# A list scheduler, single PSUM banks and 64x64 transposes in an attention and adapter kernel

## The chip, the core and the metric

The kernel runs on one core of one Trainium2 chip. The metric is the device time of one execution in microseconds (us). Five engines matter: PE multiplies matrices and writes PSUM, ACT and DVE read PSUM and do the elementwise work, POOL starts the loads, SP starts the stores. Each runs its own instructions strictly in the order in which the program gives them, and waits on semaphores for the others. PSUM has eight banks, each of 512 float32 numbers in each of 128 partitions.

## What is computed

Attention with a squared ReLU in place of the softmax (8 batches, 12 heads, 448 rows, head width 64), and behind it a mixture of eight low-rank adapters (rank 16) on the 3584 rows of 768 numbers that it gives; each row takes the two adapters with the highest gate.

```python
scores = scale * np.matmul(q, k.transpose(0, 1, 3, 2))
attn = np.maximum(scores, 0.0) ** 2 / S
x = np.matmul(attn, v)                  # then (b, s, h * d): 3584 x 768
...
logits = x @ w_gate                     # 768 -> 8
topk = np.argpartition(-logits, K, axis=1)[:, :K]          # K = 2
w = np.exp(sel); w /= w.sum(-1, keepdims=True) + 1e-09
delta[mask] += w[mask, k, None] * ((x[mask] @ A[e]) @ B[e])
out = x + delta
```

## The kernel before

**Tiling.** Two heads from each half of the twelve form a quad, so there are three quads for each batch and 24 in all. A quad's keys are cut into seven blocks of 64 rows. One block of one quad is a *slot*; there are 168. In a slot PE multiplies a block of k with all of q for four heads (`emit_qk`, L228: four 64x64 matmuls of 448 columns, which sit in the four quarters of the array), ACT takes the ReLU of the two banks of scores in one instruction of 896 columns (`emit_relu`, L238), DVE squares it (L240), and PE multiplies by v and adds into two banks `oT` (`emit_pv`, L252, four 64x64 matmuls again). After seven slots `emit_xt` copies the two banks as bf16 into `xt` (ACT L262, DVE L263), which holds the attention's result transposed.

**Transposes.** q and k of the next quad are turned by `job_transpose`: 14 matmuls against an identity, each on 128 rows and 64 columns (L112), into one bank, which DVE copies out at once (L119, 896 bf16 columns). There is one such job for q and one for k of each quad, 48 in all.

**Adapters.** `job_moe` handles two or three 128-row tiles at a time, twelve groups for 28 tiles: six matmuls for each tile give gate and first adapter factor (L133), a chain of small DVE instructions with one ACT exponential makes the weights (L145 to L166), a transpose (L175) and a copy (L180) turn the weighted factor, and for each tile two output parts of 512 and 256 columns follow: identity matmuls that bring x back (L189), the second factor in float32 (L197), the copy out (ACT L208, DVE L210), the store (SP L212).

**Order.** The loop over slots writes it out by hand: `emit_qk`, then one step of a transpose job or of `job_moe` (each `yield` ends a step), then `emit_relu`, then `emit_pv` of the slot two before (`LAG = 2`). A batch's adapter work begins when its last quad is copied out; what is left of it when the slots end is run behind them.

**Buffers.** The scores have two tiles of two banks, `oT` two banks, and transposes, gates and outputs share two banks (`ps_m`). A batch's loads go out on POOL's queue two batches ahead, in three tiles; the first batch's are cut into two slots' worth each.

Of the kernel before, what the change touches and what calls it, by code (L numbers as in the profile page):

```python
# [12 lines left out]
ALU = mybir.AluOpType  # L13

J = 7
PH = 64


@with_exitstack
def kernel(  # L20
# [21 lines left out]
    NC_ = HH // 2  # L42
    scale = 1.0 / math.sqrt(Dh)
# [3 lines left out]
    loads = ctx.enter_context(tc.tile_pool(name="loads", bufs=3))  # L47
    tpool = ctx.enter_context(tc.tile_pool(name="tpool", bufs=2))
    apool = ctx.enter_context(tc.tile_pool(name="apool", bufs=4))
    mpool = ctx.enter_context(tc.tile_pool(name="mpool", bufs=2))  # L50
    opool = ctx.enter_context(tc.tile_pool(name="opool", bufs=4))
    ps_s = ctx.enter_context(tc.tile_pool(name="ps_s", bufs=2, space=bass.MemoryType.PSUM))
    ps_o = ctx.enter_context(tc.tile_pool(name="ps_o", bufs=1, space=bass.MemoryType.PSUM))
    ps_m = ctx.enter_context(tc.tile_pool(name="ps_m", bufs=2, space=bass.MemoryType.PSUM))
# [5 lines left out]
    identb = const.tile([128, 128], BF16)  # L60

# [5 lines left out]
    )  # L67

    batches = {}

    def load_batch(b, per_quad=False):
        tiles = [
            loads.tile([128, HH, J * Dh], BF16, name=f"{nm}n{b}", tag=f"{nm}n") for nm in "qkv"
        ]
        batches[b] = tiles
        parts = [(2 * c, 2 * c + 2) for c in range(NC_)] if per_quad else [(0, HH)]
        for s0, s1 in parts:
            for t, src in zip(tiles, (qv, kv, vv)):
                for g in range(2):
                    nc.gpsimd.dma_start(  # L80
                        out=t[g * PH : g * PH + PH, s0:s1, :], in_=src[b, g, :, s0:s1, :]
                    )
# [3 lines left out]
    load_batch(0, per_quad=True)  # L86
    nc.sync.dma_start(out=B_sb, in_=moe_B.rearrange("e r d -> (e r) d"))
    load_batch(1)
    nc.gpsimd.dma_start(
        out=awg[:, :, RE:ZW], in_=moe_w_gate.rearrange("(do di) e -> di do e", di=128)  # L90
    )
    for do in range(DO):
        nc.gpsimd.dma_start(
            out=awg[:, do, 0:RE].rearrange("p (e r) -> p e r", e=E),
            in_=moe_A[:, do * 128 : do * 128 + 128, :].transpose([1, 0, 2]),
        )

    quads = [(b, c) for b in range(B) for c in range(NC_)]
    NQ = len(quads)
    qkT = {}  # L100

    def misc(name):
        return ps_m.tile([128, 512], F32, name=name, tag="misc")


    def job_transpose(qi, which):
        b, c = quads[qi]
        src = batches[b][which]
        ps = ps_m.tile([128, J * 128], BF16, name=f"tp{which}_{qi}", tag="misc")
        for j in range(J):  # L110
            for sl in range(2):
                nc.tensor.transpose(  # L112
                    ps[sl * PH : sl * PH + PH, j * 128 : j * 128 + 128],
                    src[:, 2 * c + sl, j * Dh : j * Dh + Dh],
                    identb,
                )
        yield
        sb = tpool.tile([128, J, 2, PH], BF16, name=f"{'qk'[which]}T{qi}", tag=f"{'qk'[which]}T")
        nc.vector.tensor_copy(sb.rearrange("p j a s -> p (j a s)"), ps)  # L119
        qkT[qi, which] = sb  # L120

    def out_rows(m, bp):

        b = 2 * bp + m // J
        return out[b * S : b * S + S, :].rearrange("(p j) f -> j p f", j=J)[m % J]

    def job_moe(bp, tiles_):
        T = len(tiles_)
        c0 = [bp * 2 * S + 128 * i for i in tiles_]
        z = misc(f"z{bp}_{tiles_[0]}")  # L130
        for t in range(T):
            for do in range(DO):
                nc.tensor.matmul(  # L133
                    out=z[:, t * ZW : t * ZW + ZW],
                    lhsT=xt[:, do, c0[t] : c0[t] + 128],
                    rhs=awg[:, do, :],
                    start=(do == 0),
                    stop=(do == DO - 1),
                )
        yield  # L140
        z3 = z[:, : T * ZW].rearrange("p (t w) -> p t w", t=T)
        lg = z3[:, :, RE:ZW]
        mx = mpool.tile([128, 3, 8], F32, name=f"mx{bp}_{tiles_[0]}", tag="mx")
        for t in range(T):
            nc.vector.max(mx[:, t, :], z[:, t * ZW + RE : t * ZW + ZW])  # L145
        sub = mpool.tile([128, 3, E], F32, name=f"sub{bp}_{tiles_[0]}", tag="sub")
        nc.vector.tensor_tensor(
            sub[:, :T], lg, mx[:, :T, 0:1].to_broadcast([128, T, E]), op=ALU.subtract
        )
        w = mpool.tile([128, 3, E], F32, name=f"w{bp}_{tiles_[0]}", tag="w")  # L150
        nc.scalar.activation(w[:, :T], sub[:, :T], ACTF.Exp)
        mask = mpool.tile([128, 3, E], F32, name=f"mask{bp}_{tiles_[0]}", tag="mask")
        nc.vector.tensor_tensor(
            mask[:, :T], lg, mx[:, :T, 1:2].to_broadcast([128, T, E]), op=ALU.is_ge
        )
        yield
        nc.vector.tensor_mul(w[:, :T], w[:, :T], mask[:, :T])
        ws = mpool.tile([128, 3], F32, name=f"ws{bp}_{tiles_[0]}", tag="ws")
        nc.vector.reduce_sum(ws[:, :T], w[:, :T], axis=mybir.AxisListType.X)
        nc.vector.reciprocal(ws[:, :T], ws[:, :T])  # L160
        nc.vector.tensor_tensor(
            w[:, :T], w[:, :T], ws[:, :T, None].to_broadcast([128, T, E]), op=ALU.mult
        )
        zp = mpool.tile([128, 3, E, R], F32, name=f"zp{bp}_{tiles_[0]}", tag="zp")
        for t in range(T):
            nc.vector.tensor_tensor(  # L166
                zp[:, t],
                z[:, t * ZW : t * ZW + RE].rearrange("p (e r) -> p e r", e=E),
                w[:, t, :, None].to_broadcast([128, E, R]),
                op=ALU.mult,  # L170
            )
        yield
        zt = misc(f"zt{bp}_{tiles_[0]}")
        for t in range(T):
            nc.tensor.transpose(  # L175
                zt[:, t * 128 : t * 128 + 128], zp[:, t].rearrange("p e r -> p (e r)"), identf
            )
        yield
        zT = mpool.tile([128, 3 * 128], F32, name=f"zT{bp}_{tiles_[0]}", tag="zT")
        nc.scalar.copy(zT[:, : T * 128], zt[:, : T * 128])  # L180
        yield
        pend = None
        for t in range(T):
            osb = opool.tile([128, D], F32, name=f"o{bp}_{tiles_[t]}", tag="o")
            for part in range(2):
                d0, nd = (0, 4) if part == 0 else (4, 2)
                o = misc(f"o{part}_{bp}_{tiles_[t]}")
                for i in range(nd):
                    nc.tensor.matmul(  # L189
                        out=o[:, i * 128 : i * 128 + 128],  # L190
                        lhsT=xt[:, d0 + i, c0[t] : c0[t] + 128],
                        rhs=identb,
                        start=(i == 0),
                        stop=False,
                        skip_group_check=True,
                    )
                nc.tensor.matmul(  # L197
                    out=o[:, : nd * 128],
                    lhsT=zT[:, t * 128 : t * 128 + 128],
                    rhs=B_sb[:, d0 * 128 : (d0 + nd) * 128],  # L200
                    start=False,
                    stop=True,
                    skip_group_check=True,
                )
                yield
                dst = osb[:, d0 * 128 : (d0 + nd) * 128]
                if part == 0:
                    nc.scalar.copy(dst, o[:, : nd * 128])  # L208
                else:
                    nc.vector.tensor_copy(dst, o[:, : nd * 128])  # L210
                    for hh in range(2):
                        nc.sync.dma_start(  # L212
                            out=out_rows(2 * tiles_[t] + hh, bp),
                            in_=osb[hh * PH : hh * PH + PH, :],
                        )


    sc, at2, oT = {}, {}, {}

    def emit_qk(n):  # L220
        qi, j = divmod(n, J)
        qT, kT = qkT[qi, 0], qkT[qi, 1]
        s = ps_s.tile([128, 2, 512], F32, name=f"s{n}", tag="s")
        sc[n] = s
        for sl in range(2):
            r0 = sl * PH
            for a in range(2):
                nc.tensor.matmul(  # L228
# [118 lines left out]
```

## Time and profile before

| | before |
|---|---|
| median of 3 runs | 277.51 us (277.43 to 278.75) |
| the profiled execution | 275.26 us |
| its span | 273.5 us |
| busy: PE, ACT, DVE | 205.1, 177.7, 169.2 us |
| first ReLU starts | 9.94 us |
| last v matmuls start | 249.55 us |
| mean granted TensorE clock | 0.931 of 2.4 GHz |

An engine's busy time counts an instruction from its start to its end, and instructions that follow closely on one engine overlap, so what an instruction holds up its engine for is read from the distance between two starts where nothing waits. Lines as L238 are lines of the kernel before; `a<-s` reads "writes a, reads s".

### The profile page before, as it was taken

The numbers are of one execution on the slowest core, as the hardware profiler recorded it, in microseconds if no ns is written. First come the engines' busy times: TensorE is split into PE (matmuls) and PEld (weight loads), VectorE is DVE, ScalarE is ACT, GpSimd is POOL, SyncE is SP. The second block draws the span as 40 slices with busy tenths as digits, with TensorE's granted clock in tenths as the row PEclk, the third lists the DMA queues.
The fourth block names the chain that finished last, engine by engine and source line by source line (L and its number), as shares of the span: only waits on it lengthen the run. The fifth ranks groups of instructions, "written<-read, shape, count | busy, mean of one in ns | idle before, by whom it ended". The sixth has DMA issues, their size and how long they took to land.

```text
span 273.5 us, 6096 instructions
## 1 busy us (share of the span) xinstructions
PE 205.1 (75%) x2492; PEld 100.3 (37%) x2492; DVE 169.2 (62%) x397; ACT 177.7 (65%) x245; POOL 45.2 (17%) x73
## 2 busy tenths in 40 slices
PE   0877759976795997898697687788686866789762
PEld 0433424433343344434344334334233433334331
DVE  0588866586867657756877767755746666463230
ACT  1488957786786576767777787676736776664120
POOL 8975732101110103001110100000000000000000
PEclk9999997999999599599999999799959979979799
DMA  7999999998193188716692642022200400403244
GB/s 130 186 181 182 112 203 205 220 228 139 21 211 89 9 149 145 119 37 123 128 188 72 112 97 60 2 59 60 59 2 6 111 0 2 115 2 84 89 116 115
DMA packets 31067, 28.51 MB, mean 104 GB/s; under 512 B 8896, under 2 KB 27328, under 8 KB 31040
## 3 DMA queue, kind: packets, MB, share of 16 engines
q0 software_dynamic: 26416, 16.73, 49.3%
q1 hardware_dynamic: 4624, 11.41, 15.4%
q8 instruction: 19, 0.31, 0.5%
q14 instruction: 8, 0.07, 0.1%
HBM read 33.84 MB, written 11.01 MB: 164 GB/s over the span
## 4 chain that ended last, share of the span: by engine, by line
PE 44%; DVE 21%; ACT 19%; issue 8%; POOL 4%; DMA 2%; ACTq 0%; POOLq 0%
ACT a L238 15%; PE o L197 15%; PE oT L252 10%; DVE a L240 9%; PE s L228 7%; PE o L189 6%; ACT o L208 3%; DVE kT L119 3%; DMA qn<-in_q_dram 2%; DVE xt L263 2%; PE tp L112 2%; PE zt L175 2%; DVE zp L166 2%; POOL qn L80 2%; PE z L133 2%
## 5 line engine op out<-in xcount | busy, mean ns | idle before, releaser
L238 ACT ACTIVATE a<-s 128x896 bf16<-128x896 f32 x168 | 148.6, 921 | 43.9 <-PE s L228 42.9
L240 DVE TENSOR_TENSOR a<-a 128x896 bf16<-128x896 bf16 x168 | 103.5, 623 | 76.0 <-ACT a L238 74.7
L252 PE MATMUL oT<-a,vn 64*64 64x448 bf16 x672 | 71.6, 390 | 13.5 <-DVE a L240 4.8
L228 PE MATMUL s<-qT,kT 64*64 64x448 bf16 x672 | 68.0, 381 | 10.9 <-ACT a L238 10.2
L197 PE MATMUL o<-B_sb,zT 128*128 128x512 f32 (+1 forms) x112 | 53.0, 559 | 0.5 <-ACT zT L180 0.5
L252 PEld LDWEIGHTS <-vn 64*64 64x64 bf16 x672 | 23.5, 108 | 61.2 <-issue 49.8
L228 PEld LDWEIGHTS <-kT 64*64 64x64 bf16 x672 | 24.3, 112 | 18.9 <-issue 14.9
L189 PE MATMUL o<-identb,xt 128*128 128x128 bf16 x168 | 20.5, 236 | 12.0 <-ACT o L208 8.3
L208 ACT COPY o<-o 128x512 f32<-128x512 f32 x28 | 16.5, 589 | 16.6 <-PE o L197 16.6
L189 PEld LDWEIGHTS <-xt 128*128 128x128 bf16 x168 | 12.3, 104 | 34.3 <-issue 29.5
L80 POOL DMA_DIRECT2D vn<-in_v_dram x20 | 13.0, 666 | 64.7 <-PE s L228 46.0
L112 PE MATMUL tp<-identb,qn 128*64 128x128 bf16 x336 | 15.8, 241 | 6.6 <-DMA qn<-in_q_dram 6.6
L197 PEld LDWEIGHTS o<-B_sb,zT 128*128 128x128 f32 x112 | 18.8, 210 | 0.8 <-ACT zT L180 0.8
L175 PE MATMUL zt<-identf,zp 128*128 128x128 f32 x28 | 7.2, 354 | 15.2 <-DVE zp L166 15.2
L119 DVE COPY qT<-tp 128x896 bf16<-128x896 bf16 x24 | 14.8, 615 | 5.8 <-PE tp L112 5.8
L210 DVE COPY o<-o 128x256 f32<-128x256 f32 x28 | 11.7, 418 | 10.6 <-PE o L197 10.6
L80 POOL DMA_DIRECT2D qn<-in_q_dram x20 | 13.2, 671 | 30.4 <-PE tp L112 28.6
L112 PEld LDWEIGHTS <-qn 128*64 128x64 bf16 x336 | 11.6, 121 | 15.7 <-issue 8.4
L133 PE MATMUL z<-awg,xt 128*128 128x136 bf16 x168 | 12.7, 223 | 4.3 <-DVE kT L119 2.4
L263 DVE CAST xt<-oT 128x448 bf16<-128x448 f32 x24 | 14.8, 618 | 1.7 <-PE oT L252 1.7
L112 PE MATMUL tp<-identb,kn 128*64 128x128 bf16 x336 | 15.1, 233 | 0.3 <-DMA kn<-in_k_dram 0.3
L119 DVE COPY kT<-tp 128x896 bf16<-128x896 bf16 x24 | 14.8, 618 | 0.6 <-PE tp L112 0.6
(25 smaller groups left out, 89.6 us busy)
## 6 DMA issues: line engine op xcount, KB each, us to landing
out_dram<-o SPq DMA_DIRECT2D x56, 192.0 KB, 2.7
qn<-in_q_dram POOLq DMA_DIRECT2D x14, 336.0 KB, 6.5
kn<-in_k_dram POOLq DMA_DIRECT2D x14, 336.0 KB, 7.5
vn<-in_v_dram POOLq DMA_DIRECT2D x14, 336.0 KB, 6.0
qn<-in_q_dram POOLq DMA_DIRECT2D x6, 112.0 KB, 4.5
kn<-in_k_dram POOLq DMA_DIRECT2D x6, 112.0 KB, 4.5
vn<-in_v_dram POOLq DMA_DIRECT2D x6, 112.0 KB, 4.7
B_sb<-in_moe_B_dram SPq DMA_DIRECT2D x1, 384.0 KB, 3.3
```

Source lines behind the costliest of these rows:

```text
L80: nc.gpsimd.dma_start(out=t[g * PH : g * PH + PH, s0:s1, :], in_=src[b, g, :, s0:s1, :])
L112: nc.tensor.transpose(ps[sl * PH : sl * PH + PH, j * 128 : j * 128 + 128], src[:, 2 * c + sl, j * Dh : j * Dh + Dh], identb,)
L119: nc.vector.tensor_copy(sb.rearrange("p j a s -> p (j a s)"), ps)
L133: nc.tensor.matmul(out=z[:, t * ZW : t * ZW + ZW], lhsT=xt[:, do, c0[t] : c0[t] + 128], rhs=awg[:, do, :], start=(do == 0), stop=(do == DO ...
L189: nc.tensor.matmul(out=o[:, i * 128 : i * 128 + 128], lhsT=xt[:, d0 + i, c0[t] : c0[t] + 128], rhs=identb, start=(i == 0), stop=False, ski ...
L197: nc.tensor.matmul(out=o[:, : nd * 128], lhsT=zT[:, t * 128 : t * 128 + 128], rhs=B_sb[:, d0 * 128 : (d0 + nd) * 128], start=False, stop=True,
L208: nc.scalar.copy(dst, o[:, : nd * 128])
L228: nc.tensor.matmul(out=s[a * PH : a * PH + PH, sl, 0:S].rearrange("p (j s) -> p j s", j=J), lhsT=kT[r0 : r0 + PH, j, a, :], rhs=qT[r0 : r0 ...
L238: nc.scalar.activation(a1, sc[n][:, :, 0:S], ACTF.Relu, scale=relu_scale)
L240: nc.vector.tensor_mul(a2, a1, a1)
L252: nc.tensor.matmul(out=oT[qi][g][sl * PH : sl * PH + PH, 0:S], lhsT=vn[r0 : r0 + PH, 2 * c + sl, j * Dh : j * Dh + Dh], rhs=at2[n][r0 : r0 ...
L263: nc.vector.tensor_copy(xt[:, NC_ + c, b * S : b * S + S], oT[qi][1][:, 0:S])
```

## The change

The slots' loop is replaced by a list of operations with their costs, engines, buffers and PSUM banks; a planner (`schedule`) runs through it once when the program is built, and the instructions are issued in the order of its planned start times. The chip still runs a fixed order.

- **Planner.** It keeps a time for each engine, picks ready operations, prefers q-k matmuls, then v matmuls and transposes of the form 64x64, and puts adapter work (`mode="128"`) between where the planned ReLUs cover it. Copies out of PSUM go to ACT or DVE, whichever is free.
- **Banks.** One PSUM tile of eight banks; four are for scores, four for all else, given and returned one by one. The ReLU of a slot is two instructions of 448 columns, each of which returns its bank.
- **Transposes.** 28 matmuls of 64x64 for each job in place of 14 of 128x64, in the four quarters of the array, into two banks; two DVE copies of 448 columns in place of one of 896.
- **Adapters.** Ten groups (eight of three tiles, two of two) in place of twelve. The zp product is one DVE instruction for a group. Output: each pair of tiles has three banks of 512 columns and three copies out, and the second factor goes in pieces of 256 columns (84 in place of 56 matmuls). Stores are 63 in place of 56 DMAs.
- **Last batch.** Its rows are cut into two halves of 224 columns with 21 slots each, so there are 147 whole and 42 half slots.
- **Loads.** The second batch is loaded in parts too. The adapters' first factor comes in rows of 96 numbers and PE puts it in place with a selection matrix (72 small matmuls).

```diff
+BANKS = {"s": [0, 1, 2, 3], "m": [4, 5, 6, 7]}
+DEFER = 3
...
+        att = sorted(
+            (o for o in c if o.mode == "64" and not (o.kind == "tp" and o.rank > next_q)),
+            key=lambda o: (o.kind == "pv", o.kind == "tp", seq[id(o)]),
+        )
+        late = [o for o in c if o.kind == "tp" and o.rank > next_q]
+        fill = [o for o in c if o.mode != "64"]
+
+        cover = max(free["ACT"], t) + sum(o.dur["ACT"] for o in relus)
+        if mode == "64" and att:
+            return att[0]
+        if fill:
+            f = fill[0]
+            if not att or att[0].kind != "qk" or t + f.dur[e] + switch + 0.55 <= cover + SLACK:
+                return f
+        return (att or fill or late)[0]
...
+    ps = psum.tile([128, 8, 512], F32)
...
+        def mm():
+            for j in range(J):
+                for g in range(2):
+                    r = slice(g * PH, g * PH + PH)
+                    for sl in range(2):
+                        nc.tensor.transpose(
+                            bank(m, g).bitcast(BF16)[sl * PH : sl * PH + PH, j * PH : j * PH + PH],
+                            T[b, w][r, 2 * c + sl, j * Dh : j * Dh + Dh],
+                            identb[r, r],
+                        )
...
+        r0 = op(ACT, act(W), AL, lambda: fn(0), deps=[qk_ops[n]], after=prev, kind="relu",
+                take=("a1",), free=[(qk_ops[n], 0)])
+        r1 = op(ACT, act(W), AL, lambda: fn(1), deps=[qk_ops[n]], after=r0, kind="relu", free=[(qk_ops[n], 1)])
...
+    for o in schedule(ops):
+        o.fn()
...
-    LAG = 2
-    run(job_transpose(0, 0))
-    run(job_transpose(0, 1))
...
-        if n < total:
-            emit_relu(n)
-        if 0 <= n - LAG < total:
-            emit_pv(n - LAG)
-    for g in todo:
-        run(g)
```

**The first group of gates on DVE.** Here `a2` is a slot's square, `kT` a transposed k, `mx` to `zp` the gate chain. Before:

```order
L240 TENSOR_TENSOR a2_24_662<-a1_24_660 128x896
L119 COPY kT4_673<-tp1_4_645 128x896
L145 MAX mx0_0_675<-z0_0_611 128x8 x3
L147 TENSOR_TENSOR sub0_0_679<-z0_0_611,mx0_0_675 128x24
L153 TENSOR_TENSOR mask0_0_683<-z0_0_611,mx0_0_675 128x24
L240 TENSOR_TENSOR a2_25_687<-a1_25_685 128x896
L157 TENSOR_TENSOR w0_0_681<-w0_0_681,mask0_0_683 128x24
L159 TENSOR_REDUCE ws0_0_699<-w0_0_681 128x3
L160 RECIPROCAL ws0_0_699<-ws0_0_699 128x3
L161 TENSOR_TENSOR w0_0_681<-w0_0_681,ws0_0_699 128x24
L166 TENSOR_TENSOR zp0_0_703<-z0_0_611,w0_0_681 128x128 x3
L240 TENSOR_TENSOR a2_26_709<-a1_26_707 128x896
```

The same group on DVE after the change:

```order
L497 MAX mx_0_940<-ps_91 128x8 x3
L428 TENSOR_TENSOR a2_26_948<-a1_26_918 128x896
L504 TENSOR_TENSOR sub0_965<-ps_91,mx_0_940 128x24
L513 TENSOR_TENSOR mask0_967<-ps_91,mx_0_940 128x24
L428 TENSOR_TENSOR a2_27_973<-a1_27_938 128x896
L520 TENSOR_TENSOR wt0_979<-wt0_979,mask0_967 128x24
L523 TENSOR_REDUCE ws0_989<-wt0_979 128x3
L428 TENSOR_TENSOR a2_28_991<-a1_28_963 128x896
L528 RECIPROCAL ws0_989<-ws0_989 128x3
L463 CAST xt_92<-ps_91 128x448
L532 TENSOR_TENSOR wt0_979<-wt0_979,ws0_989 128x24
L428 TENSOR_TENSOR a2_29_1036<-a1_29_987 128x896
```

One square stood inside the chain before; four stand between its links now.

**The same group's exponential on ACT** (`w`, now `wt`), among the ReLUs (`a1`). Before:

```order
L238 ACTIVATE a1_23_630<-s23_604 128x896
L238 ACTIVATE a1_24_660<-s24_640 128x896
L151 ACTIVATE w0_0_681<-sub0_0_679 128x24
L238 ACTIVATE a1_25_685<-s25_668 128x896
L238 ACTIVATE a1_26_707<-s26_693 128x896
L238 ACTIVATE a1_27_724<-s27_715 128x896
L180 COPY zT0_0_737<-zt0_0_720 128x384
```

On ACT after the change, where "x2" marks the two halves of a slot:

```order
L413 ACTIVATE a1_24_879<-ps_91 128x448 x2
L413 ACTIVATE a1_25_901<-ps_91 128x448 x2
L413 ACTIVATE a1_26_918<-ps_91 128x448 x2
L413 ACTIVATE a1_27_938<-ps_91 128x448 x2
L413 ACTIVATE a1_28_963<-ps_91 128x448
L510 ACTIVATE wt0_979<-sub0_965 128x24
L413 ACTIVATE a1_28_963<-ps_91 128x448
L413 ACTIVATE a1_29_987<-ps_91 128x448 x2
```

The exponential stood one ReLU behind the maxima's inputs; it now stands four slots further on, and the zT copy has left this stretch of ACT for DVE.

**The end of PE's list.** Before, behind the last v matmul (L252), there are 24 gate matmuls, 4 transposes, 30 identity matmuls and 10 of L197, five tiles' worth. They end so:

```order
L197 MATMUL o_3_5_4129<-B_sb,zT_5_4126 128x512
L189 LDWEIGHTS xt
L189 MATMUL o_3_5_4136<-identb,xt 128x128
```

After the change (v matmuls are L441) there stand behind the last of them 24 gate matmuls, 10 transposes, 64 identity matmuls and 32 second-factor matmuls of 256 columns:

```order
L441 MATMUL ps<-a_188_4758,vn_2919 64x224
L592 LDWEIGHTS xt
L592 MATMUL ps<-identb,xt 128x128
L592 LDWEIGHTS xt
L592 MATMUL ps<-identb,xt 128x128
L600 MATMUL ps<-B_sb,zT_4306 128x256
L558 MATMUL ps<-identf,zp_4312 128x128
L480 LDWEIGHTS xt
L480 MATMUL ps<-awg,xt 128x136
```

Output work of 32 / 3, between ten and eleven tiles, has moved behind the attention, where five tiles stood.

On ACT the changed kernel has 336 ReLUs of 448 columns, 20 xt copies of 448 and 6 of 224, 22 output copies of 512, 4 zT copies and 10 exponentials; on DVE 147 squares of 896 and 42 of 448, 96 transposed copies of 448, 22 and 6 xt copies, 20 output copies.

## Rows read from the trace of the kernel before

**Rows 1.** The page's first part: busy time, share of the span, instructions.

```profile
PE 205.1 (75%) x2492; PEld 100.3 (37%) x2492; DVE 169.2 (62%) x397; ACT 177.7 (65%) x245; POOL 45.2 (17%) x73
```

**Rows 2.** Windows: stretch, length, each engine's busy time (count), granted clock, DMA.

```profile
9.90:30.00 20.10, 15.62 (x240) 7.86 (x237) 15.77 (x27) 17.80 (x23) 13.49 (x20) 1.00 2.24 166
...
60.00:247.40 187.40, 147.23 (x1827) 70.94 (x1827) 124.39 (x295) 131.72 (x182) 13.10 (x20) 0.92 0.41 79
```

**Rows 3.** The same stretches for the ReLU's line L238 alone.

```profile
9.90:30.00 20.10, 17.29 (x21) 1.00 2.24 166
60.00:247.40 187.40, 112.65 (x127) 0.92 0.41 79
```

**Rows 4.** Waits: who waited for whom, us in total, times, longest.

```profile
ACT a L238 <- PE s L228: 42.9, 53, 7.9
...
ACT w L151 <- DVE sub L147: 17.5, 12, 1.7
```

**Rows 5.** Timeline at a gate: start, length, engine, what, idle time before.

```profile
108.28 0.22 ACT L151 ACTIVATE w<-sub 128x24 f32<-128x24 f32 x1 [1.67 <-DVE sub L147]
108.40 2.56 ACT L238 ACTIVATE a<-s 128x896 bf16<-128x896 f32 x3
...
109.35 0.59 PE L228 MATMUL s<-qT,kT 64*64 64x448 bf16 x4 [1.66 <-ACT a L238]
```

**Rows 6.** Windows behind that gate: the granted clock is the last number but two.

```profile
112.00:117.00 5.00, 5.00 (x48) 2.27 (x52) 3.36 (x6) 3.55 (x5) 0.00 (x0) 0.59 0.35 57
```

**Rows 7.** Timeline of ACT: the first ReLUs, and a copy between ReLUs.

```profile
9.94 1.73 ACT L238 ACTIVATE a<-s 128x896 bf16<-128x896 f32 x2 [7.92 <-PE s L228]
...
14.23 4.16 ACT L238 ACTIVATE a<-s 128x896 bf16<-128x896 f32 x5 [0.50 <-PE s L228]
18.23 0.58 ACT L262 CAST xt<-oT 128x448 bf16<-128x448 f32 x1
18.64 0.99 ACT L238 ACTIVATE a<-s 128x896 bf16<-128x896 f32 x1
```

**Rows 8.** Tile and line views: durations in ns, least, median, most.

```profile
L262 ACT CAST xt<-oT x24: 523/532/580, 18.2 to 250.0; 128x448 bf16<-128x448 f32 x24
```

**Rows 9.** Timeline of DVE: three instructions without a wait.

```profile
104.42 0.61 DVE L263 CAST xt<-oT 128x448 bf16<-128x448 f32 x1
104.95 0.61 DVE L119 COPY qT<-tp 128x896 bf16<-128x896 bf16 x1
105.48 0.61 DVE L240 TENSOR_TENSOR a<-a 128x896 bf16<-128x896 bf16 x1
```

**Rows 10.** Timeline of PE: a transpose job between slots.

```profile
17.16 0.58 PE L112 MATMUL tp<-identb,qn 128*64 128x128 bf16 x14
17.68 0.38 PE L252 MATMUL oT<-a,vn 64*64 64x448 bf16 x4
17.89 0.36 PE L228 MATMUL s<-qT,kT 64*64 64x448 bf16 x4
```

**Rows 11.** The durations of one transpose matmul, same columns as rows 8.

```profile
L112 PE MATMUL tp<-identb,qn x28: 219/219/244, 17.2 to 24.6; 128*64 128x128 bf16 x28
```

**Rows 12.** Timeline of PE: two output parts between v matmuls.

```profile
246.98 0.38 PE L252 MATMUL oT<-a,vn 64*64 64x448 bf16 x4
...
248.53 0.38 PE L252 MATMUL oT<-a,vn 64*64 64x448 bf16 x4
...
249.55 0.38 PE L252 MATMUL oT<-a,vn 64*64 64x448 bf16 x4
```

**Rows 13.** Timeline of PE: twelve gate matmuls, and the last tile's two output parts.

```profile
251.85 0.87 PE L133 MATMUL z<-awg,xt 128*128 128x136 bf16 x12
...
266.52 0.38 PE L189 MATMUL o<-identb,xt 128*128 128x128 bf16 x4
...
267.77 0.65 PE L197 MATMUL o<-B_sb,zT 128*128 128x256 f32 x2
```

**Rows 14.** Timeline: one DMA's issue on SP's queue.

```profile
0.74 0.39 SPq L87 DMA_DIRECT2D B_sb<-in_moe_B_dram  x1
```

More of the change, by code (lines that the diff above doesn't have):

```diff
@@ L67 @@
     )
[L69 to L82, printed above, removed]
+    UB = [1] * (B - 1) + [2]
@@ new lines @@
+    order = []
+    for b in range(B):
+        if UB[b] == 1:
+            order += [(b, 0, c, j) for c in range(NC_) for j in range(J)]
+        else:
+            order += [(b, u, c, j) for u in range(UB[b]) for c in range(NC_) for j in range(J)]
+    NS = len(order)
+    first_use, last_use = {}, {}
+    for n, (b, u, c, j) in enumerate(order):
+        first_use.setdefault((b, c), n)
+        last_use[b, c] = n
+    loaded, tp_ops = {}, {}
+    qk_ops, relu_ops, sq_ops, pv_ops, xt_ops = {}, {}, {}, {}, {}
@@ new lines, in sq, with fn, pv @@
+    def sq(n):
+        W = width(order[n][0])
+        def fn():
+            a2 = new("a2", ("a2", n), [128, 2, W], BF16)
+            nc.vector.tensor_mul(a2, T["a1", n], T["a1", n])
+        return op(DVE, dve(2 * W, 1.92), DL, fn, deps=relu_ops[n], take=("a2",), give=("a1",))
+    def pv(n):
+        b, u, c, j = order[n]
+        W = width(b)
+        def fn():
+            vn = T[b, 2]
+            for g in range(2):
+                r0 = g * PH
+                for sl in range(2):
+                    nc.tensor.matmul(
+                        out=bank(head, g)[sl * PH : sl * PH + PH, :W],
+                        lhsT=vn[r0 : r0 + PH, 2 * c + sl, j * Dh : j * Dh + Dh],
+                        rhs=T["a2", n][r0 : r0 + PH, sl, :],
+                        start=(j == 0),
+                        stop=(j == J - 1),
+                    )
+        wait = [sq_ops[n], loaded[b, 2, c]]
+        if j == 0:
+            wait += [sq_ops[n + DEFER]]
+        o = op(PE, 0.194 / UB[b], PL, fn, mode="64", kind="pv", deps=wait, after=pv_ops.get(n - 1),
+               banks=("m", 2) if j == 0 else None, give=("a2",))
+        head = o if j == 0 else pv_ops[n - j]
+        return o
@@ L218 @@
[L218 to L228, printed above, removed]
-                    out=s[a * PH : a * PH + PH, sl, 0:S].rearrange("p (j s) -> p j s", j=J),
-                    lhsT=kT[r0 : r0 + PH, j, a, :],
-                    rhs=qT[r0 : r0 + PH, :, a, :],
-                    start=True,
-                    stop=True,
-                )
@@ new lines, in gate, with f_zt @@
+        o_wn = op(DVE, 0.09, DL, f_wn, deps=[o_rec], rank=GATE)
+        o_zp = op(DVE, dve(n * RE), DL, f_zp, deps=[o_wn], free=[(zops[0], 0)], give=("w",), take=("zp",),
+                  rank=GATE)
+        zts = []
+        for t in range(n):
+            def f_zt(t=t):
+                nc.tensor.transpose(
+                    bank(zts[0])[:, t * 128 : t * 128 + 128],
+                    T["zp", g0][:, t].rearrange("p e r -> p (e r)"),
+                    identf,
+                )
+            zts.append(op(PE, 0.235, PL, f_zt, mode="128", kind="fill", deps=[o_zp],
+                          after=zts[-1] if zts else None, banks=("m", 1) if t == 0 else None,
+                          give=("zp",) if t == n - 1 else ()))
```

656 lines of the change are left out of this document (466 added, 190 removed).

## The prediction

> **What bounds the kernel now.** I read the page's first part first: no engine is full [rows 1]. PE is busy for 75% of the span, ACT for 65%, DVE for 62%. So the bound is the order in which they wait for one another, and I looked for a stretch in which they wait less. The windows have one. From 9.9 to 30 us there is attention and transposing but no adapter work yet, and 21 ReLUs pass in 20.1 us, 0.957 us a slot; from 60 to 247.4 us 127 pass in 187.4 us, 1.476 us a slot [rows 2, 3]. The half microsecond between the two is what adapter work costs a slot, though PE and ACT have room for it.
>
> The waits say how. ACT waited 42.9 us for q-k matmuls and 17.5 us for the maxima ahead of its exponential [rows 4]. The timeline shows one case: the exponential stands in ACT's list ahead of a ReLU and waits 1.67 us for DVE; the ReLU behind it frees its bank late, and PE stands still for 1.66 us [rows 5]. After that PE's granted clock is 0.59 for five microseconds, most of them at the lower level of 1.2 GHz, with PE busy throughout [rows 6]. So one wait of ACT is paid three times.
>
> **What an instruction holds its engine for.** Five ReLUs take 4.16 us and two take 1.73, so one more costs 0.81; the xt copy of 448 columns between ReLUs ends 0.42 us after the ReLU ahead of it, the next ReLU 0.82 after that [rows 7]. DVE's 896 bf16 or 448 float32 columns stand 0.53 us apart [rows 9]. On PE a transpose job holds the engine for 0.52 us, a group of four q-k or v matmuls for 0.21, here taken as 0.20 [rows 10].
>
> **ACT after the change.** The ReLU is split. That half the columns cost half the time has no row; the nearest is the copy of the same width, 0.42 us behind a ReLU and 0.532 alone [rows 7, 8]. I take 0.42, because ReLUs will stand behind one another; the other end is a rival below. 336 x 0.42 = 141.1 us. The xt copies give 20 x 0.42 + 6 x 0.21 = 9.7, output copies of 512 columns (0.42 x 512 / 448 = 0.48) 22 x 0.48 = 10.6, the exponentials 10 x 0.12 = 1.2 (the distance at 108.28 [rows 5]), four zT copies 1.4. Sum 164.0; six output copies and a few small ones, 4.0, come after the last ReLU. That leaves **160 us between the first ReLU and the last**.
>
> **PE after the change**, same stretch: 294 groups of 448 columns x 0.20 = 58.8; 84 groups of 224, between 0.10 (half) and 0.20, taken 0.13: 10.9. The transposes have no row of their form. They stream half as many columns (28 x 64 over four quarters against 14 x 128 over two), which from 0.52 could leave some 0.33; if each costs what one costs now, 0.52 / 14 = 37 ns, 28 cost 1.04. I take 0.5, nearer the low end, because the groups of four in rows 10 do sit side by side: 48 x 0.5 = 24, what the 48 jobs cost now. Gate and selection matmuls: 192 x 0.0725 (0.87 / 12 [rows 13]) = 13.9. Transposes of zp: 18 x 0.2 = 3.6, 0.2 being some three gate matmuls. Output pieces: between two v groups a part of 256 columns costs 249.55 - 248.53 - 0.20 = 0.82 with both changes of form, a part of 512 costs 248.53 - 246.98 - 0.20 = 1.35, so 256 more cost 0.53 [rows 12]. Some pieces will stand alone and some in rows: 52 x 0.7 = 36.4. Sum **148 us**.
>
> **DVE after the change**: squares 147 x 0.53 + 42 x 0.30 = 90.5; transposed copies 96 x 0.30 = 28.8 (half of 0.53 and a little: two instructions have two beginnings, some 3 us more than now); xt 22 x 0.53 + 6 x 0.30 = 13.5; output 20 x 0.61 = 12.2; gate chains, zT and the placing of the first factor some 17, an estimate from distances of 0.1 for a small one and 0.45 for a wide one. Sum 162, of which 10 after the last ReLU: **152 us**.
>
> So three engines come out within 8%, ACT longest, and the order decides how near to 160 the stretch comes. In the stretch without adapter work ACT held 21 x 0.82 + 2 x 0.42 = 18.1 of 20.1 us, 90% [rows 2, 3]. I take that 90% for the whole: the planner puts a fill of 0.7 us only where planned ReLUs of up to 1.64 us (two slots of scores) cover it, four squares now stand inside the gate chain, and the exponential is four slots behind its inputs, so the wait of 1.67 us has what it waited for done long before. What is late next is then a q-k group behind a fill or behind a transpose job. 160 / 0.90 = **177.8 us**.
>
> **Ends.** The first ReLU starts at 9.94 us [rows 7]; loads, identity and first transposes ahead of it are the same, and I leave it at 9.9 (the first job now has twice the matmuls: nothing to 0.5 us more). POOL's queue has a selection matrix and two more DMAs before the second batch, whose parts are needed only some 20 slots in; I cost that at nothing while the loads keep ahead, else at a few microseconds in that batch. From the last ReLU to the last v matmul 0.8 us. **The tail grows**: 32 pieces are 10.7 tiles, and the last tile takes from 266.52 to 267.77 + 0.65, 1.90 us [rows 13], so 20.3; 24 gate matmuls 1.7, ten transposes 2.0. From 268.42 to the span's end it is 5.1 us now; the last pair stores eight pieces in place of two, and six issues at 0.39 on SP's queue [rows 14] make it 7.4. Tail 31.4 us.
>
> **The sum**: 9.9 + 177.8 + 0.8 + 31.4 = 219.9 of span, and 1.8 that lie around it in the profiled execution (275.26 against 273.5): **222 us** against 275.26. The median of before is 277.51, 0.8% above the execution profiled; I let the forecast stand for the median, since 0.8% is small beside its range.
>
> **The rivals.**
>
> *ACT is full.* If the planned order leaves ACT no gap, the stretch is 160 and the time 204 us. For it: four banks handed back one by one free a score bank half a ReLU earlier. Against: DVE and PE would have to be 95% and 92% full beside it.
>
> *The halves cost more than half.* If ReLUs of 448 columns hold ACT for 0.47, halfway to 0.532, the stretch grows by 336 x 0.05 / 0.9 = 18.7 and the time is 240; at 0.532 alone it is 264 [rows 8]. For it: nothing shows two such ReLUs in a row. Against: the 0.42 in rows 7. The Trainium skill has a rule that speaks for this rival (ScalarE: Activation LUTs, What ACT_TABLE_LOAD costs): an activation with immediate operands takes 186 ns and 0.833 ns a column, and back to back they overlap by about 93 ns. By an estimate from it 448 columns hold ACT for 0.466 us and the time would be 239; for 896 it gives 0.84, where rows 7 show 0.81, and for 448 rows 7 show 0.42, so I follow the rows and let the rule weigh in the chance.
>
> *PE takes over.* Transposes at 1.04 add 48 x 0.54 = 25.9 and output pieces all alone at 0.82 add 6.2: PE has 180, at 90% the stretch is 200 and the time 244. For it: 56 instructions a job. Against: quarters that overlap in rows 10.
>
> *The waits stay.* The planner's durations are not the chip's, and a fixed order that is wrong by a few tenths stalls as the old one did. With the old stretch of 239.6 us (9.94 to 249.55) and the longer tail, the time is 9.9 + 239.6 + 31.4 + 1.8 = 283; this rival covers 246 to 283.
>
> *Slower: the four blocks do not run at once.* If every 64x64 transpose waits for the one before, at its full 219 ns [rows 11], a job costs 28 x 0.219 = 6.1 us and PE 124 + 48 x 6.1 = 418, a time of 462. It decides from the point at which PE's stretch passes 277.5 - 43.9 = 233.6: (233.6 - 123.6) / 48 = 2.3 us a job, 82 ns a transpose. Against: q-k groups of the same form, four in 0.21 us.
>
> **How the numbers follow.** The forecast (210 to 234) has 0.53, ACT full 0.12, halves that cost more 0.15, PE taking over 0.10, waits that stay 0.06, blocks one after another 0.04. A measurement of this kernel tells 0.5% from no change. Of the waits that stay 0.03 are faster by more, 0.02 within it and 0.01 slower, so faster has 0.53 + 0.12 + 0.15 + 0.10 + 0.03 = 0.93, same 0.02, slower 0.01 + 0.04 = 0.05. The range goes from the full ACT, 204, to the upper rivals' 246: outside lie half of the full ACT (0.06), the dear end of the halves (0.04), and the last two rivals (0.10).
>
> **What would show it.** In the changed kernel's profile: two halves of a ReLU 0.42 us apart; a pace near 1.06 us a slot between first and last ReLU and ACT held for 90% of it; ACT's wait for maxima gone; a transpose job at 0.33 to 1.04 us; a tail near 31 us with PE busy in it; a clock nearer full, since PE stands still less. The forecast is wrong if halves stand 0.47 apart or more, if q-k matmuls still keep ACT waiting for tens of microseconds, or if the tail is well over 35 us.

## The result, and the profile of the changed kernel

| | before | changed |
|---|---|---|
| median | 277.73 us (277.43 to 278.75, 4 runs) | 223.92 us (222.41 to 224.97, 4 runs) |
| changed / before | | 0.805 (95% interval 0.800 to 0.811) |
| the profiled execution, its span | 275.26, 273.5 us | 222.41, 220.6 us |
| mean granted TensorE clock | 0.931 | 0.986 |

The forecast was 222 us with a span of 219.9. Ratios here and below come from undisturbed executions alone, so they can differ by one or two per cent from the quotient of two medians; where variants of the changed kernel are compared with one another, their medians are used.

The page's first part and its row of the granted clock, which answer to [rows 1]:

```profile
PE 195.6 (89%) x3460; PEld 119.4 (54%) x3460; DVE 171.8 (78%) x440; ACT 176.3 (80%) x399; POOL 49.0 (22%) x82
...
PEclk9999999999996999999999999999999999999997
```

ACT has nearly the busy time that it had before, in a span that is 53 us shorter: the change took idle time away, not work. The windows show where. The first is from the first ReLU's start to the last one's end, the second from there to the end. The columns are length, then busy time and instructions of PE, weight loads, DVE, ACT and POOL, granted clock, DMA share, GB/s.

```profile
9.37:189.40 180.03, 169.91 (x3227) 99.70 (x3222) 157.71 (x401) 170.08 (x387) 40.35 (x63) 0.99 0.72 125
189.40:220.60 31.20, 23.07 (x174) 18.15 (x174) 12.46 (x34) 4.97 (x12) 0.00 (x0) 0.96 0.55 155
```

In the first, ACT is busy for 170.08 of 180.03 us, 94%. PE is busy just as long here, but its busy time is not work alone, as the experiment with the ReLU in one piece shows. The waits of ACT, which answer to [rows 4] (waiting line, releaser, us in total, times, longest):

```profile
ACT a L413 <- PE ps L384: 11.3, 10, 7.4
ACT osb L625 <- PE ps L600: 10.7, 6, 3.5
...
ACT a L411 <- PE ps L384: 2.4, 7, 0.5
ACT wt L510 <- DVE sub L504: 1.9, 2, 1.2
```

Of the 11.3 us for q-k matmuls 7.35 lie ahead of the first ReLU, as 7.9 of the 42.9 did before, so some 4 are left of 35, and 2.4 for the half slots. The wait for the maxima's difference fell from 17.5 to 1.9. Of the 10.7 us for output copies all but 0.2 lie behind the last ReLU, where ACT has little else to do.

The timeline of ACT (start, us, engine, line, what, how many, and the idle time ahead with its releaser):

```profile
9.37 6.22 ACT L413 ACTIVATE a<-ps 128x448 bf16<-128x448 f32 x14 [7.35 <-PE ps L384]
...
86.06 0.66 ACT L463 CAST xt<-ps 128x448 bf16<-128x448 f32 x1
86.48 3.76 ACT L413 ACTIVATE a<-ps 128x448 bf16<-128x448 f32 x8
89.88 0.78 ACT L463 CAST xt<-ps 128x448 bf16<-128x448 f32 x1
...
188.86 0.54 ACT L411 ACTIVATE a<-ps 128x448 bf16<-128x448 f32 x1 [0.16 <-PE ps L384]
```

One half alone takes 0.54 us and the first fourteen in a row take 6.22, so one more costs (6.22 - 0.54) / 13 = 0.437 us. The eight at 86.48 agree: they end at 90.24, 3.52 behind the copy ahead of them, 0.44 each, and their starts are (89.88 - 86.48) / 8 = 0.425 apart. The forecast had 0.42. The timeline of PE, for a transpose job and for the tail:

```profile
25.74 0.41 PE L355 MATMUL ps<-identb,qn 64*64 64x64 bf16 x28 [0.28 <-DVE awg L324]
25.97 0.55 PE L384 MATMUL ps<-qT,kT 64*64 64x448 bf16 x4
...
190.28 0.39 PE L441 MATMUL ps<-a,vn 64*64 64x224 bf16 x8
...
212.08 0.65 PE L600 MATMUL ps<-B_sb,zT 128*128 128x256 f32 x2
```

The 28 transposes begin at 25.74 and the next group at 25.97, so this job holds PE for 0.23 us, not 0.5. That is the price where nothing is in the way. Of the 48 jobs 17 run so, with 0.20 to 0.22 us from the first start to the last; the others take longer, most of them with a break ahead of the first matmul on the second bank, and the median of all is 0.40. The jobs of the old form, in the first run below, have 0.36. The last v matmuls begin at 190.28, which leaves 220.6 - 190.28 = 30.3 us of tail; PE's part of it ends at 212.73.

### The profile page after: what moved, and what is told of

The parts are those of the page before. It is cut to its first block, busy times and chain, and to the rows that moved or that the text cites. A ratio compares the mean times of both kernels' runs of the same rounds, so it can differ in the third digit from the quotient of the medians.

```text
span 220.6 us, 8355 instructions
## 1 busy us (share of the span) xinstructions
PE 195.6 (89%) x3460; PEld 119.4 (54%) x3460; DVE 171.8 (78%) x440; ACT 176.3 (80%) x399; POOL 49.0 (22%) x82
## 4 chain that ended last, share of the span: by engine, by line
PE 50%; ACT 24%; DVE 12%; issue 6%; DMA 2%; POOL 1%; ACTq 0%; DVEq 0%; POOLq 0%
ACT a L413 21%; PE ps L600 15%; PE ps L384 12%; PE ps L441 11%; DVE a L428 6%; PE ps L592 5%; PE ps L355 4%; ACT xt L463 3%; DVE qT L364 2%; DMA kn<-in_k_dram 2%; PE ps L480 2%; DVE kT L364 1%; DVE xt L463 1%; ACT osb L625 1%; DVE osb L625 1%
## 5 line engine op out<-in xcount | busy, mean ns | idle before, releaser
L413 ACT ACTIVATE a<-ps 128x448 bf16<-128x448 f32 x294 | 137.7, 659 | 12.8 <-PE ps L384 11.3
L428 DVE TENSOR_TENSOR a<-a 128x896 bf16<-128x896 bf16 (+1 forms) x189 | 103.8, 570 | 19.1 <-ACT a L413 12.8
L384 PE MATMUL ps<-qT,kT 64*64 64x448 bf16 (+1 forms) x756 | 88.8, 352 | 7.0 <-DVE kT L364 3.1
L441 PE MATMUL ps<-a,vn 64*64 64x448 bf16 (+1 forms) x756 | 51.3, 341 | 1.0 <-DVE kT L364 0.5
L600 PE MATMUL ps<-B_sb,zT 128*128 128x256 f32 x168 | 52.0, 407 | 0.1
L441 PEld LDWEIGHTS <-vn 64*64 64x64 bf16 x756 | 26.2, 108 | 10.2 <-issue 4.5
L600 PEld LDWEIGHTS ps<-B_sb,zT 128*128 128x128 f32 x168 | 26.3, 191 | 3.7 <-issue 2.6
L625 ACT COPY osb<-ps 128x512 f32<-128x512 f32 x22 | 14.1, 643 | 14.6 <-PE ps L600 10.7
L411 ACT ACTIVATE a<-ps 128x448 bf16<-128x448 f32 x42 | 21.4, 556 | 3.1 <-PE ps L384 2.4
L364 DVE COPY qT<-ps 128x448 bf16<-128x448 bf16 x48 | 16.9, 384 | 6.6 <-PE ps L355 6.4
L592 PE MATMUL ps<-identb,xt 128*128 128x128 bf16 x168 | 18.8, 220 | 0.2
L364 DVE COPY kT<-ps 128x448 bf16<-128x448 bf16 x48 | 17.2, 383 | 1.3 <-PE ps L355 1.3
L274 POOL DMA_DIRECT2D kn<-in_k_dram x24 | 15.5, 666 | 4.6 <-PE ps L384 2.5
```

Source lines behind the costliest of these rows:

```text
L274: nc.gpsimd.dma_start(out=T[b, w][g * PH : g * PH + PH, s0:s1, :], in_=(qv, kv, vv)[w][b, g, :, s0:s1, :],)
L364: nc.vector.tensor_copy(T[nm, b, c][:, g, :], bank(m, g).bitcast(BF16)[:, : J * PH])
L384: nc.tensor.matmul(out=bank(o, sl)[a * PH : a * PH + PH, : width(b)].rearrange("p (j s) -> p j s", j=J), lhsT=kT[r0 : r0 + PH, a, j * PH : ...
L411: nc.scalar.activation(a1, two(qk_ops[n], W), ACTF.Relu, scale=relu_scale)
L413: nc.scalar.activation(a1[:, sl], bank(qk_ops[n], sl)[:, :W], ACTF.Relu, scale=relu_scale)
L428: nc.vector.tensor_mul(a2, T["a1", n], T["a1", n])
```

## The experiments

The theory: the time falls because the planned order keeps ACT full, and ACT's work sets the stretch; the small transposes and the halves of the last batch bring little. The rivals: the transposes' time on PE pays (0.23 in place of 0.52 us, 48 times, is 14 us); the batch halves shorten the tail; or the one wait of the exponential for the maxima was most of it, and moving that alone would do.

### The transposes as they were

```diff
-TPD = 0.25
+TPD = 0.52
...
-                for g in range(2):
-                    r = slice(g * PH, g * PH + PH)
-                    for sl in range(2):
-                        nc.tensor.transpose(
-                            bank(m, g).bitcast(BF16)[sl * PH : sl * PH + PH, j * PH : j * PH + PH],
+                for sl in range(2):
+                    nc.tensor.transpose(
+                        bank(m).bitcast(BF16)[sl * PH : sl * PH + PH, j * 128 : j * 128 + 128],
...
-                banks=("m", 2), take=(nm,), rank=first_use[b, c] - LEAD)
+                banks=("m", 1), take=(nm,), rank=first_use[b, c] - LEAD)
```

> The changed kernel with the transposes of before: 14 matmuls of 128x64 into one bank, one DVE copy of 896 columns, planned at 0.52 us a job; all else stays. Theory (ACT is the engine that is full, PE has room): PE's own work grows by 48 x (0.52 - 0.23) = 14 us, the 14 are mostly covered, 222 to 230 us. Rival (PE binds as much as ACT, the small transposes carry a good part of the gain): 14 us or more come back, 236 us or above.

Measured: 224.57 us (224.19 to 226.47). Without the blocks the kernel is as fast as with them, within 0.3%. Its windows from the first to the last ReLU, and one stall of ACT in its timeline, with the v matmuls just ahead of it:

```profile
10.23:197.90 187.67, 182.36 (x2632) 106.62 (x2629) 160.37 (x362) 170.38 (x387) 39.66 (x62) 1.00 0.70 124
```

```profile
75.18 1.51 PE L440 MATMUL ps<-a,vn 64*64 64x448 bf16 x26 [0.16 <-DVE kT L361]
...
76.32 1.42 ACT L412 ACTIVATE a<-ps 128x448 bf16<-128x448 f32 x3 [4.63 <-DVE a L427]
```

The stretch is longer (187.67 against 180.03), as PE now has more to do. What follows the last v matmuls is shorter, since 21 output pieces are left for it in place of 32: the planner moved work from one side of the last ReLU to the other. Two stalls of over 3.8 us each are part of the stretch; there the planner had put v matmuls off (26 follow one another in the timeline above), and squares and ReLUs came to a stand behind them. So a run of this one edit is not the blocks' price alone, but the sum is zero to within 0.3%.

### The last batch in one piece

```diff
-    UB = [1] * (B - 1) + [2]
+    UB = [1] * B
```

> The changed kernel with the last batch whole: 168 whole slots, no half slots. Theory (the tail is a queue of output work on PE, which the halves hardly shorten): 38 output pieces behind the last v matmul in place of 32, so the tail is some 4 us longer, 225 to 231 us. Rival (halves let the last gates start so early that much of the tail depends on them): 10 us or more longer, 234 us or above.

Measured: 224.51 us (223.45 to 225.85), just under what the theory gave. 38 pieces stand behind the last v matmuls in place of 32, yet the time is the same. The window from the first to the last ReLU shows why:

```profile
9.85:186.90 177.05, 165.49 (x3015) 95.07 (x3012) 154.56 (x377) 166.44 (x381) 39.92 (x63) 0.99 0.70 118
```

It is 3.0 us shorter than in the changed kernel, so the 42 half slots cost about what the shorter tail gives back.

### Both undone

The two edits above together: what stays of the change is the planned order, the banks one by one with the halved ReLU, the free choice of the copies' engine, and the new cut of adapters and loads.

> Two of the change's parts undone at once: transposes as before (14 of 128x64 into one bank) and the last batch whole. What is left is the planned order, the single banks, the halves of the ReLU and the free choice of ACT or DVE for copies. Theory (the order carries nearly all of the gain): 226 to 238 us, that is three quarters or more of the 54 us. Rival (the small transposes and halves carry it): 245 us or above.

Measured: 222.65 us (219.28 to 223.4), ratio 0.791 (0.782 to 0.801). My expectation was too high: with the halved ReLU both parts together are worth nothing either. The gain lies in what is left, and the next runs take a part of it apart.

### The exponential moved, in the kernel before

```diff
-        w = mpool.tile([128, 3, E], F32, name=f"w{bp}_{tiles_[0]}", tag="w")
-        nc.scalar.activation(w[:, :T], sub[:, :T], ACTF.Exp)
...
+        yield
+        w = mpool.tile([128, 3, E], F32, name=f"w{bp}_{tiles_[0]}", tag="w")
+        nc.scalar.activation(w[:, :T], sub[:, :T], ACTF.Exp)
```

The exponential becomes a step of its own, one slot later, behind one more ReLU.

> The kernel before with one step of the adapter job cut in three: the exponential is issued one slot behind the maxima, and the products one slot behind the exponential. Theory (ACT's wait for the maxima is paid by ACT, then PE, then PE's clock): the wait of 17.5 us goes below 5 and the time falls to 255 to 270 us. Rival (the wait is only moved, to DVE or to the next q-k group): 274 to 282 us.

Measured: 269.59 us, ratio 0.985 (0.964 to 1.006). The time lies at the upper end of what the theory gave, the wait is 5.8 us where it gave under 5, and the interval of the ratio is too wide to tell, so a longer comparison follows.

> The kernel before with the exponential one slot later, once more with more rounds: the first comparison left its ratio between 0.964 and 1.006. Theory: the exponential's wait is a real part of the old kernel's loss but a small one beside the wait for q-k matmuls, ratio 0.96 to 0.985. Rival: no gain, 0.99 or more.

Measured: 270.40 us (268.88 to 275.77), ratio 0.989 (0.979 to 0.999). The waits of ACT in that run, where `w` is the exponential, `a` the ReLU, `o` an output copy, and then the waits for output and zT copies before:

```profile
ACT a L239 <- PE s L229: 47.5, 55, 8.4
ACT o L209 <- PE o L198: 18.7, 20, 2.7
ACT zT L181 <- PE zt L176: 5.9, 4, 2.0
ACT w L156 <- DVE sub L147: 5.8, 7, 1.4
```

```profile
ACT o L208 <- PE o L197: 16.6, 15, 2.3
ACT zT L180 <- PE zt L175: 10.3, 9, 1.8
```

The wait for the maxima fell from 17.5 to 5.8, 11.7 us less. By the ratio the kernel gained about 1%, some 3 us, which lies between the theory's figures and the rival's. The size is uncertain: the two profiled executions are 275.26 and 270.31 us, 5.0 apart, and the medians of all executions 277.50 and 270.40, 7.1 apart, with those of the kernel before scattered from 270.95 to 280.66. ACT's wait for q-k matmuls rose from the 42.9 of [rows 4] to 47.5, and that for output copies by 2.1, while that for zT fell by 4.4: a good part of the wait came back at other instructions. Two thirds of this wait gone are worth 3 to 7 us of the 54, so it was one symptom, not the bound.

### Fills wherever one is ready

```diff
-SLACK = 0.0
+SLACK = 1000.0
```

The planner then puts adapter work between q-k groups without asking whether planned ReLUs cover it.

> The changed kernel with the planner's cover rule off: adapter work goes ahead of a ready q-k group whether or not planned ReLUs cover it. Behind the last v matmul stand 6 output pieces in place of 32. Theory (cover is what keeps ACT full): the tail falls by some 15 us, the stretch with ReLUs grows by more, and ACT waits for q-k matmuls for 20 us or more: 224 to 245 us. Rival (PE does the same work either way, and the pile behind the attention is the loss): 208 to 216 us.

Measured: 238.77 us (235.42 to 241.4), ratio 0.848 (0.839 to 0.858). The windows from the first to the last ReLU and behind it, then the waits of ACT in the first of the two:

```profile
9.84:216.60 206.76, 189.58 (x3358) 114.71 (x3355) 169.51 (x424) 173.97 (x393) 39.87 (x63) 0.99 0.68 125
216.60:233.60 17.00, 7.29 (x46) 4.95 (x45) 4.17 (x14) 1.15 (x3) 0.00 (x0) 0.85 0.33 83
```

```profile
ACT osb L625 <- PE ps L600: 17.3, 14, 2.3
ACT a L413 <- PE ps L384: 14.0, 12, 7.8
ACT a L411 <- PE ps L384: 6.0, 7, 1.6
```

The tail is 14 us shorter and the stretch 27 longer. The time is what was expected, the place only in part. ACT's waits for q-k matmuls make 20.0 us (14.0 and 6.0), but 7.8 of them lie ahead of the first ReLU, so 12.2 stand against some 6 in the changed kernel. The larger part is new: 17.3 us in output copies that stand ahead of ReLUs, for pieces that PE has not done, against 0.2. So the cover rule is worth some 13 to 15 us (the mean of the two fastest executions, 235.42 and 238.0, and the median, 238.77, each against 223.92), and it pays by leaving work for the tail, where ACT has little to do.

### Each copy on the engine that it had

```diff
-    def evac(n, fn, **kw):
+    def evac(n, fn, eng=ANY, **kw):
...
-                 deps=[pv_ops[n]], free=[(src, g)], rank=XT)
+                 deps=[pv_ops[n]], free=[(src, g)], rank=XT, eng=(ACT, DVE)[g])
...
-            evs.append(evac(512, ev, deps=[prev], after=evs[0] if evs else None,
+            evs.append(evac(512, ev, eng=(ACT, ACT, DVE)[bi], deps=[prev], after=evs[0] if evs else None,
```

The copy of zT goes to ACT too.

> The changed kernel with the copies out of PSUM tied to engines as before: the first xt bank, the zT copies and two of three output copies to ACT, the rest to DVE. Theory (ACT is full until the last ReLU and the free choice only sends a few copies to DVE): ACT gets some 12 copies more, 5 us at 0.4 each, 225 to 231 us. Rival (the free choice is what keeps ACT from waiting behind a copy whose matmuls are late): 236 us or above.

Measured: 229.67 us (228.3 to 232.03), ratio 0.838 (0.823 to 0.853). The free choice is worth 5 to 6 us. Its window behind the last ReLU is 6 us longer than in the changed kernel:

```profile
191.20:228.30 37.10, 26.51 (x220) 21.14 (x218) 9.68 (x37) 9.49 (x21) 0.00 (x0) 0.95 0.53 150
```

ACT's busy time on the page is 181.4 us against 176.3, the 5 us that the theory gave, but they lie in the tail: up to the last ReLU ACT is busy for 170.67 us, as in the changed kernel, and 38 output pieces in place of 32 stand behind the last v matmuls. With the copies tied, less adapter work goes between the ReLUs, and more of it is left for the tail.

### The planner told what a half costs

```diff
-    return n / 1400.0 + 0.075
+    return n / 1176.0 + 0.06
```

> The changed kernel with the planner's cost of an ACT instruction set to what the trace shows (0.44 us for 448 columns in place of 0.395), nothing else. Theory (the plan is robust, ACT is full either way): within 3 us of the changed kernel, 220 to 227 us. Rival (the plan's errors cost waits): 215 us or below.

Measured: 223.41 us (222.2 to 225.04), no change. The planned cost of the halves, about 0.39 us where the chip takes 0.44, is not what costs time.

### The ReLU in one piece

```diff
-    return n / 1400.0 + 0.075
+    return n / 1176.0 + 0.06
...
-                after=qk_ops.get(n - 1), banks=("s", 2, "adjacent")[: 2 + (UB[b] > 1)], ...
+                after=qk_ops.get(n - 1), banks=("s", 2, "adjacent"), ...
...
-        if UB[b] > 1:
+        if True:
```

Whole slots take one ReLU of 896 columns over two adjacent banks, which come back together.

> The changed kernel with one ReLU of 896 columns a slot in place of two of 448, both banks handed back together, and ACT's planned costs set to those of the trace (0.44 us for 448 columns, 0.82 for 896). Theory (ACT is full, so two halves at 0.44 cost 0.06 us a slot more than one whole at 0.82): 147 x 0.06 = 9 us less, 213 to 219 us. Rival (the early return of a bank is worth more than the ReLU's second beginning): 224 us or above, with ACT waiting for q-k matmuls.

Measured: 217.24 us (216.09 to 218.51), ratio 0.797 (0.784 to 0.809), 6.7 us below the changed kernel. Page, windows from the first to the last ReLU and behind it, and waits:

```profile
PE 183.1 (85%) x3460; PEld 113.5 (53%) x3460; DVE 173.7 (81%) x446; ACT 165.9 (77%) x246; POOL 48.9 (23%) x82
```

```profile
9.74:184.16 174.42, 157.60 (x3234) 93.99 (x3231) 160.11 (x415) 160.01 (x236) 39.91 (x63) 0.99 0.74 127
184.16:214.30 30.14, 22.89 (x167) 17.94 (x166) 12.01 (x26) 4.56 (x9) 0.00 (x0) 0.93 0.63 171
```

```profile
ACT a L411 <- PE ps L384: 17.5, 23, 7.7
```

```profile
PE ps L384 <- ACT a L411: 10.7, 30, 0.9
```

ACT has 10.1 us less to do in the stretch (160.01 against 170.08), and the stretch is 5.6 us shorter. The rest comes back as waits, since the banks return in pairs: PE waits 10.7 us for ReLUs (under 2 in the changed kernel) and ACT waits for q-k 7.7 us ahead of the first ReLU and 9.8 later. So ACT's work counts in the stretch, though with the other waits beside it, and the halved ReLU, which the change brought, cost more than the early bank gave. PE's busy time fell from 169.91 to 157.60 us with nearly the same matmuls (x3227 and x3234). The line of the q-k matmuls shows why, in the changed kernel and then in this run (busy us, mean ns of one, idle before them):

```profile
L384 PE MATMUL ps<-qT,kT 64*64 64x448 bf16 x588 | 78.3, 376 | 6.3 <-DVE kT L364 3.1 <-ACT a L413 1.0
```

```profile
L384 PE MATMUL ps<-qT,kT 64*64 64x448 bf16 x588 | 56.8, 376 | 11.6 <-ACT a L411 10.7 <-DVE kT L364 0.5
```

One matmul takes 376 ns in both, but their sum covers 78.3 us in the one and 56.8 in the other. Where banks come back in pairs, more of the four of a group lie side by side; where they come back singly, the matmuls follow one another with less overlap. In the trace the first and the last of a group start 0.15 us apart in the changed kernel and 0.01 us apart here (medians). So PE's share on the page, the largest of all, does not name the bound here.

### More room for fills with the whole ReLU

`SLACK = 0.8` beside the edits above.

> The kernel with whole ReLUs, with the planner's cover rule loosened by 0.8 us (SLACK 0.8). Behind the last v matmul stand 22 output pieces in place of 34. Theory (work behind the attention is only worth moving where ACT's cover pays for it): the tail falls by some 7 us and ACT loses about as much, 212 to 222 us against 217. Rival (cover rule far too strict): 210 us or below.

Measured: 218.04 us (216.44 to 219.63), the same within the runs' scatter. The limit's exact size does not matter near zero; without any limit it does.

### The transposes, the last batch and the ReLU as before

The old transposes, the last batch in one piece, and the whole ReLU. What stays is the planned order, the free choice of engines, the banks for everything but scores one by one, and the new cut of adapters and loads.

> The planned order alone: transposes as before, the last batch whole, one ReLU of 896 columns a slot with its two banks handed back together, ACT's planned cost as measured. Theory (the order is the gain, the other parts are worth nothing or cost something): as fast as the kernel with whole ReLUs alone, 212 to 221 us. Rival (with whole ReLUs ACT has room, so PE's longer transposes show): 225 us or above.

Measured: **213.77 us (212.67 to 215.06), ratio 0.768 (0.763 to 0.773)**, the fastest of all and 10 us (4.5%) below the changed kernel. Page, windows from the first to the last ReLU and behind it, waits, and a row of ReLUs:

```profile
PE 188.6 (89%) x2620; PEld 114.2 (54%) x2620; DVE 170.3 (80%) x377; ACT 163.2 (77%) x219; POOL 48.9 (23%) x82
```

```profile
10.14:185.12 174.98, 165.96 (x2423) 97.33 (x2420) 157.54 (x343) 156.74 (x208) 39.53 (x62) 1.00 0.73 127
185.12:212.70 27.58, 20.07 (x166) 15.19 (x164) 11.29 (x31) 5.13 (x11) 0.00 (x0) 0.96 0.62 172
```

```profile
ACT a L410 <- PE ps L383: 16.0, 20, 8.1
ACT a L410 <- DVE a L427: 8.1, 3, 3.8
```

```profile
13.96 2.53 ACT L410 ACTIVATE a<-ps 128x896 bf16<-128x896 f32 x3 [0.32 <-PE ps L383]
17.43 0.92 ACT L410 ACTIVATE a<-ps 128x896 bf16<-128x896 f32 x1 [0.93 <-PE ps L383]
```

Three whole ReLUs in a row take 2.53 us and one takes 0.92, so one more costs (2.53 - 0.92) / 2 = 0.81 us. ACT's work up to the last ReLU is the smallest shown, 156.74 us, yet the stretch, 174.98, is no shorter than with the whole ReLU alone, 174.42. What is shorter is the part behind it, 27.58 against 30.14 us: 26 output pieces stand behind the last v matmuls, where that run has 34. By the medians the two parts undone here bring 3.5 us beside the whole ReLU (217.24 and 213.77; the ranges do not meet), of which the profiled executions, 216.09 and 214.55, show 1.5. 8.1 us of the stretch are three stalls, two of them where the planner put v matmuls off, which a better plan could win back. No run tried that.

## Why the prediction was right, step by step

The time is right, 223.92 against 222, and each term of the sum that gives it is near; in the largest, two small errors cancel.

- **First ReLU:** 9.9 forecast, 9.37 measured. The twofold number of matmuls in the first jobs shows no cost.
- **The stretch:** 177.8 forecast, 180.03 measured. *ACT's work* was 160 in the forecast, and ACT is busy for 170.08 in the window. The surplus lies in the halves. A half in a row adds 0.437 us of busy time and not the 0.42 that I took from the copy [rows 7]: 5 to 6 us over 336 of them. And some thirty halves begin after ACT stood idle; the busy time counts each at its full 0.54 us, some 3 to 4 us more. The starts of halves in a row are 0.425 apart, as forecast. *ACT's fullness* was 90% in the forecast, taken from the stretch without adapter work; counted as the forecast counted it, by what an instruction adds in a row, ACT held some 166 of 180.03 us (160 and 336 x 0.017), 92%, and by busy time 94%. 160 / 0.90 and 166 / 0.92 are almost the same number. So the forecast's own path came, a step towards two of its rivals at once: the halves that cost more (0.437 lies a third of the way from 0.42 to 0.47) and the full ACT. That the two steps cancel is luck. The Trainium skill's rule beside the dearer halves (ScalarE: Activation LUTs, What ACT_TABLE_LOAD costs) gives 0.466 us for 448 columns and 0.84 for 896, both estimates from that page. The traces have 0.437 and 0.81, some 6% and 4% less; the half lies between the rule and my row, nearer to the row, and the measurement decides.
- **PE, 148 us:** not settled as a sum, because its busy time depends on how the matmuls overlap, 169.91 or 157.60 us for nearly the same ones. The transposes' term was too high where nothing is in a job's way: 0.23 us, below even the low end of 0.33, which would make 11 us and not 24. With the waits inside the jobs the median is 0.40. The rival of blocks one after another is refuted: 28 blocks of 0.19 us each pass in 0.41. The mistake changed nothing in the time: the run with the old transposes is as fast, which speaks against PE as the engine that set it.
- **DVE, 152 us:** 157.71 busy, of the size forecast. No run changed DVE's work alone, so that it is not the bound is not shown.
- **The wait for the maxima:** gone, as forecast (1.9 us). But I gave it too much weight: the sentence that one wait of ACT is paid three times reads one place of the timeline rightly, and taking two thirds of that wait away in the kernel before brought 1 to 3%. A stall seen once along its chain is not the stretch's price; what it releases runs into the next wait.
- **Tail:** 31.4 forecast, 30.3 measured. 32 pieces are behind the last v matmuls, as the order gave; PE's part takes 212.73 - 190.28 = 22.4 us (24.0 forecast), what follows it 7.9 (7.4 forecast).

Of the reason for the gain, the main one stands as far as runs go: a planned order covers adapter work by ReLUs and keeps ACT nearly full, and without the cover rule ACT waits. The mean granted clock is 0.986 in place of 0.931, with PE standing still less; no run separates its part. **What stays open:** of the 55 us between the kernel before and the one with both parts undone, the cover rule has about 13 to 15 and the free engines 5 to 6. If these add up, the other 35 or so lie in the order of attention work, the single banks, the new cut of the adapters' output and the earlier loads, and no run takes these apart. Only the single banks of the scores are out: where they come back in pairs the kernel is faster. The blocks in the old hand-written order were not tried.

## What to carry to other kernels

Where no engine is full and all wait in turn, look for a stretch of the same kernel in which they wait less, count the work of the engine that is longest there, and forecast that work over the fullness seen; then test each part of the change alone, since here two parts were worth nothing and a third, the ReLU in halves, cost 7 us. When an order nearly fills one engine, look first at what adds to that engine's work: here 10 us less of ACT's made the kernel 6.7 us faster, while 12 us more of PE's busy time in the stretch, with the old transposes, did not change the total. And before a time per instruction is read from a row of equal ones, make sure that no wait hides in the row: all sixteen halves at the start take 7.25 us, which would give 0.45 each, but the last two of them came 0.3 us late.

## What the runs showed of the hardware

- **64x64 transposes in the four quarters** of the array follow one another far more closely than I thought: 28 in 0.41 us with 0.19 us each, so (0.41 - 0.19) / 27 = 8 ns apart on average (the four of a set start some 3 ns apart, the next four 32 ns after them), where the 14 on 128 rows and 64 columns stood 0.52 / 14 = 37 ns apart. The row of the transposes' line groups the job at 25.74 (shortest, median and longest in ns, first and last start):

```profile
L355 PE MATMUL ps<-identb,qn x28: 186/193/213, 25.7 to 26.0; 64*64 64x64 bf16 x28
```

- **Halving an ACT instruction** on 896 PSUM columns costs some 0.06 us a pair: 0.437 for each half in a row, so 0.87 for two, against 0.81 for the whole in the last experiment and in [rows 7].
- **PE's busy time depends on how its matmuls overlap**: 169.91 and 157.60 us for 3227 and 3234 of them at the same granted clock of 0.99, so nearly all of it at 2.4 GHz.
